# T5 attention with a squared-ReLU feed-forward on one core: x of pairs 4 and 5 through the DMA transpose, x of four later pairs in one transfer, and a new table of due times

## The chip, the core and the metric

The kernel runs on one core of one Trainium2 chip. The metric is the device time of one execution in microseconds. The version before takes 360.38 us, the median of three runs (360.12 to 360.55). One profiled execution stands beside them. The kernel was scheduled by hand to within a few microseconds of its matmul work, so changes of a fraction of a per cent are what is discussed here.

## What is computed

```
scores = q @ k.T / 8                       # 8 batches, 8 heads, 576 positions, head size 64
scores = scores + bias_table[bucket(|i - j|)]
attn   = softmax(scores)                   # over the keys
x      = (attn @ v), heads put side by side  -> 4608 x 512
out    = relu(x @ w_in) ** 2 @ w_out       # w_in 512 x 2048, w_out 2048 x 512, out float32
```

Inputs and output are float32 in DRAM; inside, the kernel works in fp16 with float32 accumulation.

## The kernel before

**Attention** goes by pairs of heads. There are 32 pairs; pair p belongs to batch p // 4, so pairs 4 to 7 are batch 1, and pairs 16, 20, 24 and 28 are the first pairs of batches 4 to 7. A pair loads q and k (POOL issues those DMAs, L368), turns them so that the head size lies on partitions, and multiplies them (`scores_of`, L815 and L822; the last 64 keys in L1012). ACT takes the exponential (L997, L831, L1022), and DVE multiplies by a table of exponentiated bias (L728). `values` (L741) then multiplies by v on TensorE (L754, L761), takes a reciprocal of the row sums (L775) and writes the normalized x on DVE (L780). It does so in two parts: part 0 has three tiles of 128 positions, part 1 two (the last one half full). In batch 0 alone the parts have two and three tiles.

**x has to be turned once more**, because the feed-forward multiplies with the 512 features on partitions. There are two ways in the kernel:

- For batches 0 and 1 `x_turn` (L1068) does it on TensorE. It has five operations, one for each tile of 128 positions. Each makes four transposes (L1078), one for each pair of the batch, into one PSUM bank, and a copy on ACT (L714) or DVE (L716) brings the bank into `xt_sb`. Such an operation needs the x of all four pairs.
- From batch 2 on (`DT_X = 2`) `values` itself issues a DMA transpose from SP's queue behind each of its two parts (L793 to L799). It writes straight into `xt_sb`. There are 48 of these, two for each of 24 pairs.

**The feed-forward** goes by nine groups of 512 rows (`GT`), in `layers`. A group's first layer reads `xt_sb` (L1501, in some groups partly by seven products instead of eight, L1378; group 0 by halves, L1451). ACT and DVE apply the squared ReLU (L1530, L1540). The second layer (L1204) does with seven products of half size what would be eight. A batch has 576 rows, so group 1 (rows 512 to 1023) needs the last 64 rows of batch 0 and the first 448 rows of batch 1. Its first layer may start only when all pieces of x named in `xt_ready[1]` have landed.

**The order of the work** is set by a planner inside the kernel (`Plan.schedule`, L191). Every operation has a number, in the order in which it is made, a list of what it depends on, buffers, a price in ns and a due time. The planner walks through a modelled execution; on each engine it picks the operation that can start first, and of several that can start at once the one with the smallest due time. The instructions are then issued to each engine in that fixed order. The string `DUES` (L67 to L120) overrides the due times of about 500 operations by number (L1573 to L1575). TensorE, ACT, DVE, POOL and the queue of SP each run their list strictly in order.

Of the kernel before, what the change touches and what calls it, by code (L numbers as in the profile page):

```python
# [11 lines left out]
FP16 = mybir.dt.float16  # L12
# [21 lines left out]
DT_X = 2  # L34
RELU_DVE = 0
# [32 lines left out]
0:1620 2:1057 4:1180 10:1374 14:10158 16:8662 20:10687 22:11516 35:2669 52:4535 56:9455 58:7112 60:7916 68:10815  # L68
74:10190 76:8720 78:12175 80:15005 82:13645 84:11550 86:23580 88:22110 92:24205 94:15740 96:16365 98:5160
100:26470 102:20015 104:19280 106:20750 108:14380 110:12910 112:21375 116:24830 118:22845 120:25735 122:32560  # L70
124:28912 126:37814 128:33913 130:40556 132:37611 138:53077 140:59257 142:35621 144:56022 146:62717 148:55174
150:59442 152:57545 154:56196 156:78298 158:57307 160:47495 164:49300 166:57988 168:69667 170:53855 172:74624
174:52573 193:116470 196:82589 198:68922 200:82230 202:292670 204:92367 210:87027 214:113261 242:100900
274:107211 276:119523 282:111649 290:106325 430:180789 436:197382 438:250584 444:209080 447:199176 470:192471
496:220887 498:225440 500:217803 527:29842 528:27168 534:53417 535:54369 538:56772 539:54354 540:60089 541:57850
542:7652 548:11111 550:8057 553:10032 568:12045 573:14473 575:15118 578:13413 585:16397 598:18178 614:21930
615:22689 616:22710 619:25948 625:25934 626:29177 634:23911 635:22035 636:22362 641:27192 649:28075 653:35265
656:34983 659:28843 664:42977 671:36147 678:37745 680:37557 682:43619 692:26764 696:49415 697:77051 699:42404
702:50396 705:51612 720:49430 721:146141 729:49109 730:59630 737:58473 739:111790 740:23251 741:24529 742:22846
744:25455 746:43041 747:124773 752:20617 755:43976 760:57060 761:54459 763:47620 771:47854 772:51849 773:129366  # L80
775:48374 777:46047 779:42740 786:66406 790:62872 792:31486 798:74992 801:49147 803:61538 804:55525 805:65305
806:194213 811:64571 812:62370 829:55606 830:74008 852:80804 854:85724 858:82674 863:81398 867:83698 874:72663
878:82910 883:85677 887:68893 888:207137 892:91006 896:88734 901:75364 903:73448 907:85605 911:73890 914:95939
917:76004 918:96413 925:94537 928:89870 945:67990 946:80414 948:75587 950:67245 952:88819 981:78127 982:78920
989:89488 994:92890 1005:93482 1011:89302 1013:90614 1019:95353 1024:114015 1035:101128 1038:99231 1067:119398
1069:117655 1074:124317 1076:120546 1079:118292 1080:136781 1082:115304 1085:100217 1093:126164 1095:128386
1096:97962 1097:128084 1100:102019 1102:129303 1106:127303 1111:130634 1115:118676 1117:129752 1122:120899
1126:119722 1129:110655 1133:124513 1137:123585 1144:114735 1147:117401 1150:142607 1157:209061 1164:124814
1165:253316 1169:130366 1171:133696 1172:149728 1176:135925 1183:146398 1194:116773 1197:107201 1199:106444
1208:140568 1213:119988 1224:117192 1225:240653 1227:122452 1229:112062 1231:277079 1238:133898 1243:133447  # L90
1254:138298 1268:150015 1273:137361 1285:154673 1286:123911 1288:156589 1293:149183 1295:161760 1296:165255
1298:142184 1301:173103 1312:157945 1316:169960 1321:175132 1325:162782 1330:167105 1334:162397 1341:151871
1344:137808 1345:138678 1348:147955 1352:157383 1356:151613 1359:151655 1360:174070 1363:153941 1366:162394
1370:184432 1372:192411 1374:187205 1376:185782 1386:146887 1397:164889 1402:166927 1413:155368 1418:169097
1422:177129 1426:136922 1427:173973 1432:178937 1443:158230 1444:228059 1446:153250 1454:349338 1457:167384
1462:177010 1473:176589 1476:172655 1478:176540 1479:185500 1501:179718 1503:182250 1508:190343 1510:203005
1516:199512 1523:171343 1527:190195 1531:205450 1534:183047 1536:208496 1540:207327 1545:200160 1549:203926
1556:207389 1560:184812 1567:203181 1571:198563 1576:198936 1578:201689 1581:208725 1588:225038 1591:244956
1603:175092 1612:196147 1617:183544 1628:195491 1631:212780 1633:224396 1635:217128 1639:225517 1658:189178
1663:191367 1672:210715 1677:211394 1678:227828 1687:192179 1688:203407 1693:209674 1707:227130 1716:219200  # L100
1718:226066 1720:214927 1723:238316 1725:237862 1728:238618 1729:194614 1734:211389 1739:224576 1742:244441
1745:212768 1746:235036 1749:211379 1751:243380 1755:236163 1760:242402 1764:254767 1771:248608 1775:252775
1782:239688 1786:236303 1789:231239 1793:249320 1796:251032 1802:260804 1805:258837 1807:172350 1813:226190
1814:235218 1816:224638 1818:216417 1827:236087 1846:221877 1848:237634 1849:253782 1850:245738 1851:256163
1857:244985 1864:350531 1873:233367 1879:227859 1880:228340 1887:245518 1892:255737 1894:258771 1906:230982
1908:244937 1909:248019 1910:253722 1918:154960 1922:256387 1935:266967 1937:267963 1942:269901 1944:270198
1945:286508 1947:271205 1950:269272 1952:274893 1953:233383 1954:247394 1961:255388 1965:270026 1968:262833
1970:276519 1971:279751 1973:284808 1974:278869 1977:272671 1979:274936 1982:284959 1983:151931 1986:262274
1990:265311 1994:275938 1995:280226 1998:288907 2001:273934 2005:256374 2012:286562 2015:251154 2021:296191
2023:289373 2032:263421 2035:260356 2037:274391 2038:264239 2039:282682 2040:278169 2046:280738 2051:286535  # L110
2062:261514 2068:261952 2069:255665 2076:272292 2092:273655 2095:275739 2099:272928 2122:278929 2125:285022
2126:284839 2127:277523 2128:283181 2129:280296 2141:295193 2150:297975 2152:299266 2157:306028 2159:311561
2165:290995 2172:302812 2174:303364 2179:301973 2181:308356 2184:293569 2187:309532 2190:275380 2194:309550
2195:309256 2196:313265 2198:307321 2201:313552 2203:313106 2209:317667 2212:290350 2213:188745 2224:72572
2226:310220 2227:311767 2231:283869 2236:304785 2240:302563 2247:295321 2250:302190 2255:330506 2265:310664
2267:319453 2269:317532 2272:318235 2274:329364 2275:326890 2277:115300 2280:314656 2283:317429 2285:321158
2290:321339 2292:326200 2298:327300 2299:329122 2301:330181 2303:327337 2308:319851 2310:335293 2316:334886
2319:48914 2320:295724 2323:330893 2325:333730 2330:336969 2332:335768 2335:331254 2338:89017 2341:324215
2342:327990 2345:329056 2349:323549 2350:329628 2352:330954 2367:348049
# [146 lines left out]
def mm(n):  # L266
    return n / 2.4 + 2.5
# [11 lines left out]
def kernel(  # L279
# [425 lines left out]
    xt_ready, x_last, xt_half, every_slot = {}, {}, {}, []  # L705
# [35 lines left out]
    def values(p, part, qt0, nq, pb, deps, T, after):  # L741
# [48 lines left out]
        if b >= DT_X:  # L790
            c = (b % XB) * S + 128 * qt0
            t = P.add(
                {"SP": 1320.0},  # L793
                lambda: io(
                    nc.sync.dma_start_transpose(
                        out=xt_sb[:, hp, c : c + 128 * nq].rearrange("p (t d) -> p t d", d=128), in_=xs[xb.slot][:, qt0 : qt0 + nq, :].rearrange("p t d -> p (t d)")
                    )
                ),
                [o, x_last.get((hp, 1 - part))] + xt_free(b * S + 128 * (qt0 + nq)), [xb], T - 2000,  # L799
            )  # L800
            t = x_last[hp, part] = P.land((128 * nq, 25.0), [t], [xb], SPARE[1])
            end = b * S + min(128 * (qt0 + nq), S) - 1
            for g_ in range((b * S + 128 * qt0) // GT, end // GT + 1):
                xt_ready.setdefault(g_, []).append(t)
# [114 lines left out]
    def pair(p):  # L919
# [116 lines left out]
        else:  # L1036
# [28 lines left out]
            values(p, part, qt0, nq, pb, bands + list(exps.values()), T, after) for part, qt0, nq in ((0, 0, 3), (1, 3, 2))  # L1065
        ]

    def x_turn(b, norms):  # L1068
        xb = [x_bufs[4 * b + hp] for hp in range(4)]
        T = nominal(4 * b + 3)  # L1070
        for qt in range(5):
            n = 128 if qt < 4 else 64
            bank = Buf(r_g)

            def tr(qt=qt, bank=bank):
                ps = g_ps[bank.slot].bitcast(FP16)
                for kk in range(4):
# [531 lines left out]
```

## Time and profile before

| | before |
|---|---|
| median of three runs | 360.38 us (360.12 to 360.55) |
| the profiled execution: its time | 360.5 us |
| its span, first to last instruction | 358.7 us |
| TensorE busy (PE) | 346.4 us, 97% of the span |
| VectorE (DVE), ScalarE (ACT), GpSimd (POOL) | 297.5, 272.6, 170.6 us |
| granted TensorE clock | 1.0 throughout |
| x transposes on TensorE (L1078) | 40 |
| x transposes by DMA (L795) | 48 |

The profiled execution's time is 1.8 us more than its span; that rest lies outside of the first and the last instruction. "PE" is the matmul pipeline, "PEld" the load of weights into it, "SPq" the queue of SyncE. A line number is a line of the kernel before. Ends of matmuls are modelled, so the distance between the starts of neighbours tells more of a matmul's price than its own duration.

### The profile page before, as it was taken

The page shows a single profiled execution, that of the slowest core. Times are in us where ns is not written, and L with a number is a line of the kernel's source. Part 1 is how long each engine was busy: PE and PEld are TensorE (multiplying, and loading weights), DVE is VectorE, ACT ScalarE, POOL GpSimd, SP SyncE. Part 2 cuts the span into 40 slices and gives each one's busy share as a digit, 9 for nine tenths or more (in the row PEclk, how much of TensorE's full clock was granted, in tenths as well). Part 3 has the DMA queues.
Part 4 walks back from the last instruction along what each step waited for, and adds up shares of the span by engine and source line. Part 5 has one row for each costly group of instructions (what it writes and reads, how often), then busy time and mean ns, then how long its engine had stood idle before and what let it go on. Part 6 is the DMA issues. An engine that isn't in the chain of part 4 may idle for free.

```text
span 358.7 us, 10742 instructions
## 1 busy us (share of the span) xinstructions
PE 346.4 (97%) x4290; PEld 262.0 (73%) x4290; DVE 297.5 (83%) x673; ACT 272.6 (76%) x435; POOL 170.6 (48%) x289
## 2 busy tenths in 40 slices
PE   3988999999999999999999999999999999999996
PEld 3666788775587558877788568755867887888885
DVE  4888999666996799768896899798988798899993
ACT  4898997589966988678976887689889833899830
POOL 8886679698995896158478456221000000000000
PEclk9999999999999999999999999999999999999999
DMA  9999999999999999799999999863410032010023
GB/s 172 151 147 198 193 150 154 190 156 192 175 130 165 223 158 112 119 163 198 84 134 164 186 126 133 150 121 72 61 44 15 18 97 68 27 63 33 23 66 117
DMA packets 162210, 44.37 MB, mean 124 GB/s; under 512 B 145520, under 2 KB 162160, under 8 KB 162160
## 3 DMA queue, kind: packets, MB, share of 16 engines
q0 software_dynamic: 74208, 14.53, 54.6%
q1 hardware_dynamic: 87696, 28.86, 44.3%
q8 instruction: 33, 0.54, 0.6%
q10 hardware_dynamic: 256, 0.30, 0.3%
q14 instruction: 17, 0.14, 0.1%
HBM read 36.94 MB, written 9.44 MB: 129 GB/s over the span
## 4 chain that ended last, share of the span: by engine, by line
PE 88%; DMA 7%; POOL 2%; ACT 1%; issue 1%; DVE 0%; POOLq 0%
PE f L1204 31%; PE f L1501 20%; PE f L761 10%; PE st L815 8%; PE f L1378 7%; DMA w_in_sb<-in_moe_w_in_dram 5%; PE f L1451 3%; PE st L1378 3%; PE f L754 3%; PE st L1012 2%; DMA ks<-in_k_dram 2%; POOL va L368 2%; PE f L822 1%; PE f L1078 1%; POOL ks L368 0%
## 5 line engine op out<-in xcount | busy, mean ns | idle before, releaser
L997 ACT ACTIVATE pt<-st 128x1024 f16<-128x1024 f32 x112 | 111.1, 1031 | 23.0 <-PE st L815 22.8
L1501 PE MATMUL f<-xt,w_in_sb 128*128 128x512 f16 (+4 forms) x416 | 77.2, 330 | 0.0
L728 DVE TENSOR_TENSOR pt<-pt,tb_sb 128x512 f16<-128x512 f16 (+3 forms) x108 | 61.9, 581 | 12.6 <-ACT pt L997 9.3
L368 POOL DMA_DIRECT2D ks<-in_k_dram x79 | 55.9, 719 | 15.1 <-DMA kt<-ks 10.4
L1204 PEld LDWEIGHTS <-g 128*128 128x128 f16 x576 | 55.1, 98 | 7.6 <-issue 0.8
L368 POOL DMA_DIRECT2D qs<-in_q_dram x79 | 55.5, 712 | 8.1 <-DMA qt<-qs 6.2
L1530 ACT ACTIVATE rt<-f 128x512 f16<-128x512 f32 x80 | 47.3, 608 | 14.1 <-PE f L1501 12.7
L1501 PEld LDWEIGHTS <-w_in_sb 128*128 128x128 f16 x416 | 37.1, 98 | 26.7 <-issue 2.5
L761 PE MATMUL f<-va,pt 128*128 128x65 f16 x1280 | 53.2, 193 | 0.3 <-DMA va<-in_v_dram 0.3
L761 PEld LDWEIGHTS <-pt 128*128 128x128 f16 x1280 | 49.8, 97 | 1.3 <-issue 0.5
L1204 PEld LDWEIGHTS <-s 128*128 128x128 f16 x432 | 41.1, 98 | 5.8 <-issue 0.8
L1232 DVE SCALAR_TENSOR_TENSOR y<-f,y 128x512 f32<-128x512 f32 (+1 forms) x48 | 31.8, 665 | 12.5 <-PE f L1204 11.7
L815 PE MATMUL st<-qt,kt 64*128 64x512 f16 (+1 forms) x288 | 40.4, 361 | 1.0 <-DVE qt L716 0.6
L1540 DVE TENSOR_TENSOR g<-rt 128x512 f16<-128x512 f16 x80 | 34.3, 433 | 6.2 <-ACT rt L1530 5.3
L1204 PE MATMUL f<-wt,g 128*128 128x256 f16 x288 | 35.6, 273 | 0.0
L754 PE MATMUL f<-vm,pm 128*128 128x130 f16 x160 | 35.5, 222 | 0.0
L1204 PE MATMUL f<-w_out_sb,s 128*128 128x256 f16 x288 | 35.3, 273 | 0.0
L1204 PE MATMUL f<-w_out_sb,g 128*128 128x256 f16 x288 | 34.7, 273 | 0.1
L780 DVE TENSOR_TENSOR x<-f,r 128x384 f16<-128x384 f32 (+1 forms) x64 | 30.9, 485 | 0.9
L645 POOL CAST va<-f 128x512 f16<-128x512 f32 x24 | 16.7, 702 | 30.8 <-DMA f<-in_v_dram 17.5
L974 POOL COPY kz<-kt 64x64 f16<-64x64 f16 x55 | 19.4, 354 | 20.2 <-DMA kt<-ks 17.1
L831 ACT ACTIVATE pt<-f 128x256 f16<-128x256 f32 x64 | 22.9, 404 | 5.9 <-PE f L822 4.5
(112 smaller groups left out, 532.4 us busy)
## 6 DMA issues: line engine op xcount, KB each, us to landing
out_dram<-y SPq DMA_DIRECT2D x34, 256.0 KB, 2.8
f<-in_v_dram SPq DMA_DIRECT2D x24, 256.0 KB, 4.9
ks<-in_k_dram POOLq DMA_DIRECT2D x48, 64.0 KB, 5.2
qs<-in_q_dram POOLq DMA_DIRECT2D x48, 64.0 KB, 4.4
w_in_sb<-in_moe_w_in_dram POOLq DMA_DIRECT2D x4, 512.0 KB, 10.7
w_out_sb<-in_moe_w_out_dram POOLq DMA_DIRECT2D x4, 512.0 KB, 8.9
ks<-in_k_dram POOLq DMA_DIRECT2D x7, 144.0 KB, 5.6
qs<-in_q_dram POOLq DMA_DIRECT2D x7, 144.0 KB, 5.5
```

What stands on the lines that cost most here:

```text
L368: lambda: io(eng.dma_start(out=out_(), in_=in_())),
L728: io(nc.vector.tensor_tensor(out=a, in0=a, in1=t, op=MULT))
L754: nc.tensor.matmul(ps[:, i, :, :], pm[:, c : c + 128], vm[:, hp, :, 0:65], start=True, stop=False)
L761: nc.tensor.matmul(ps[:, i, e, :], pt[:, (2 * jt + e) * S + c : (2 * jt + e) * S + c + 128], va[:, jt, 2 * hp + e, 0:65], start=False, sto ...
L815: nc.tensor.matmul(banks[i][:, e, :], kt[rw[e], ts(jt, 128)], qt[rw[e], ds(q0, n)], start=True, stop=True)
L997: nc.scalar.activation(out=p5(pts[pb.slot])[:, jt, :, 0:512], in_=sets_ps[st.slot], func=EXPF, scale=SCALE)
L1204: nc.tensor.matmul(home[bf.slot][:, ts(s_, HALF)], left(c, s_), right(c), start=(c == 0 and (s_ == 0 or apart) and (own or i not in before ...
L1232: nc.vector.scalar_tensor_tensor(out=dst, in0=ps, scalar=OSC, in1=ys[y[plus].slot][:, cs], op0=MULT, op1=mybir.AluOpType.add,)
L1378: nc.tensor.matmul(ps()[:, ds(HALF * f + a, z - a)], left()[:, kk, ts(f, 128)], right(a, z)[:, kk, :], start=(first_ and f == 0 and a == 0 ...
L1501: nc.tensor.matmul(g_ps[bank.slot][:, a:z], w_in_sb[:, kk, ts(nt, 128)], xt_sb[:, kk, c : c + z - a], start=(kk == 0), stop=(kk == 3),)
L1530: io(nc.scalar.activation(out=rts[rb.slot], in_=g_ps[bank.slot], func=RELUF))
L1540: nc.vector.tensor_tensor(out=gs[gb1.slot][:, nt, :], in0=rts[rb.slot], in1=rts[rb.slot], op=MULT)
```

## The change

It has three parts.

1. Two sets of pair numbers are new: `X_DMA = (4, 5)` and `X_ONCE = (16, 20, 24, 28)`.
2. Pairs 4 and 5, the first two pairs of batch 1, send x through the DMA transpose as batches 2 to 7 do. `x_turn` turns the pairs that are left. In batch 1 these are two, and as an operation still fills a bank of four transposes, it takes two tiles at a time: three operations of 4, 4 and 2 transposes take the place of five of 4. In batch 0 nothing is different.
3. Pairs 16, 20, 24 and 28 issue one DMA transpose of all five tiles behind the part that comes second, instead of one of three tiles and one of two.

All due times that `DUES` overrides are new: 467 entries stand where 502 stood. As the change makes and removes operations, their numbers shift: by 2 to 8 within batch 1, by 4 behind it, and from pair 16 on step by step back to minus 4. Up to number 762 they are the same.

```diff
+X_DMA = (4, 5)
+X_ONCE = (16, 20, 24, 28)
...
         o = P.add({"DVE": dve(nq * 128)}, norm, [o], [bank, rb, xb], T - 2000)
-        if b >= DT_X:
-            c = (b % XB) * S + 128 * qt0
+        if p in X_ONCE:
+            if not part:
+                x_first[p] = o
+                return o
+        a_, n_ = (0, 5) if p in X_ONCE else (qt0, nq)
+        if b >= DT_X or p in X_DMA:
+            c = (b % XB) * S + 128 * a_
             t = P.add(
                 {"SP": 1320.0},
                 lambda: io(
                     nc.sync.dma_start_transpose(
-                        out=xt_sb[:, hp, c : c + 128 * nq]..., in_=xs[xb.slot][:, qt0 : qt0 + nq, :]...
+                        out=xt_sb[:, hp, c : c + 128 * n_]..., in_=xs[xb.slot][:, a_ : a_ + n_, :]...
                     )
                 ),
-                [o, x_last.get((hp, 1 - part))] + xt_free(b * S + 128 * (qt0 + nq)), [xb], T - 2000,
+                [o, x_first.get(p), x_last.get((hp, 1 if p in X_ONCE else 1 - part))] + xt_free(b * S + 128 * (a_ + n_)),
+                [xb], T - 2000,
             )
...
     def x_turn(b, norms):
-        xb = [x_bufs[4 * b + hp] for hp in range(4)]
+        turn = [hp for hp in range(4) if 4 * b + hp not in X_DMA]
+        xb = [x_bufs[4 * b + hp] for hp in turn]
+        k0, nk = turn[0], len(turn)
+        wide = 4 // nk
         T = nominal(4 * b + 3)
-        for qt in range(5):
-            n = 128 if qt < 4 else 64
+        for qt in range(0, 5, wide):
+            qts_ = range(qt, min(qt + wide, 5))
+            n = min(128 * wide, S - 128 * qt)
...
-                for kk in range(4):
-                    io(nc.tensor.transpose(ps[:, ts(kk, 128)], xs[xb[kk].slot][:, qt, :], id_sb))
+                for i in range(nk):
+                    for j, t_ in enumerate(qts_):
+                        io(nc.tensor.transpose(ps[:, i, ts(j, 128)], xs[xb[i].slot][:, t_, :], id_sb))
...
-            deps = [n_[0 if qt < (2 if b < HALVES else 3) else 1] for n_ in norms]
+            early = 2 if b < HALVES else 3
+            deps = [norms[hp][w] for hp in turn for w in range(2) if (qts_[0] < early if w == 0 else qts_[-1] >= early)]
```

A few of the due times that matter for what follows, by the operation's number (which is the same before and after for these): 590 and 594, the two sets of score products of part 0 of pair 2, 5300 before, 14785 and 15933 after; 760, the product with v of part 0 of pair 4, 57060 before, 70746 after; 763, that of part 1, 47620 before, 51633 after.

## The prediction

> **What bounds the kernel now.** I read the page's busy times first, then the busy times cut into three stretches, then the waits of TensorE, then the chain of work that ended last around the transposes that go, and at last the rows of the DMA transposes. The page:
>
> ```profile
> PE 346.4 (97%) x4290; PEld 262.0 (73%) x4290; DVE 297.5 (83%) x673; ACT 272.6 (76%) x435; POOL 170.6 (48%) x289
> ```
>
> TensorE is busy in nearly all of the span, and no other engine comes near. Three stretches (PE, weight load, DVE, ACT and POOL busy, granted clock, DMA):
>
> ```profile
> 0.00:34.33 34.33, 25.24 (x511) 19.02 (x511) 25.17 (x78) 27.93 (x46) 27.54 (x53) 1.00 1.32 166
> 34.33:355.49 321.16, 321.06 (x3780) 243.02 (x3780) 271.86 (x595) 244.69 (x390) 143.04 (x236) 1.00 0.97 119
> 355.49:358.70 3.21, 0.06 (x1) 0.00 (x0) 0.42 (x1) 0.00 (x0) 0.00 (x0) 0.98 0.48 161
> ```
>
> From 34.33 us to 355.49 us PE rests for 0.10 us of 321.16. That stretch is a list of matmuls one behind the other, at full clock; it becomes shorter only by instructions that go. Ahead of it PE rests for 9.1 us, behind it lie 3.2 us of reading, storing and landing. The waits of PE (total, times, longest):
>
> ```profile
> PE f L419 <- DMA id_sb<-c_id: 4.4, 1, 4.4
> PE f L1451 <- DMA w_in_sb<-in_moe_w_in_dram: 1.3, 1, 1.3
> PE f L947 <- ACT ex_sb L424: 1.3, 1, 1.3
> PE st L815 <- DVE qt L716: 0.6, 1, 0.6
> PE f L947 <- DVE qt L716: 0.4, 1, 0.4
> PE f L761 <- DMA va<-in_v_dram: 0.3, 1, 0.3
> PE st L815 <- ACT pt L864: 0.3, 1, 0.3
> ...
> ```
>
> All of them lie in the first 34 us. Behind the first there are 4.2 us that another order could at best win back.
>
> **Part by part: the transposes of batch 1.** The chain of work that ended last runs through all 20 of them (start, length, what); these are the pieces:
>
> ```profile
> 74.10 0.22 PE f L1078 x4
> ...
> 75.19 0.67 PE f L1078 x12
> ...
> 80.09 0.22 PE f L1078 x4
> ```
>
> 20 transposes cost 0.22 + 0.67 + 0.22 = 1.11 us, 0.056 us each. The change makes 4 + 4 + 2 = 10 instead of 20, in one stretch without any cover, so **-0.56 us** on the path.
>
> A rule speaks against this part: in the Trainium skill, "VectorE: DVE Perf Modes", section "Rules for kernel authors", a 128x128 transpose belongs on TensorE where PSUM may take the result, and its section on the three paths gives 390 ns there against 1309 ns for the DMA. By these figures ten would be 3.9 us of TensorE, seven times what the chain shows; the rule compares one transpose alone with another, and here TensorE is what is full. It is right on latency, which the second rival takes up.
>
> **The copies.** Five copies out of PSUM become three. In the stretch from 75 to 80 us DVE is busy for 2.52 us of 5 and ACT for 4.26; one of 512 columns takes 0.42 us on DVE or 0.59 us on ACT. Two less give about 1 us to engines that don't set the end: nothing. Were ACT the bound, it would be worth up to 1.2 us.
>
> **Four more DMA transposes** for pairs 4 and 5 go into SP's queue among the q and k transposes of batch 2. The rows of the existing ones:
>
> ```profile
> L795 SPq DMA_TRANSPOSE xt<-x x48: 1168/1206/2377, 89.7 to 298.6; - x48
> DMA to landing us min/median/max: 2.3/4.1/6.9
> ```
>
> Each holds SP for 1.2 us and waits there for its norm on DVE; the q and k transposes and stores behind it wait too. Between 55.35 + 1.34 = 56.7 us and 62.2 us SP's queue issues nothing, so the room is there. Who waits for those q and k transposes are scores of batch 2, and PE has other work meanwhile. I take nothing; without that cover it would be 4 x 1.2 = 4.8 us of delay at the worst.
>
> **One transfer instead of two** for pairs 16, 20, 24 and 28 takes four issues of 1.2 us off SP, which isn't a bound, and holds the x of part 0 back until part 1 is ready. What covers this are the other three pairs of the same batch, which the feed-forward needs as well: batch 4's first x transposes are issued at 169.8 us, the layer that reads them starts at 196.7 us. Nothing; without the cover one landing, 4.1 us (up to 6.9).
>
> **The due times** reorder each queue, and the trace of before can't show the new order. Above: a better order can win at most the 4.2 us of waits in the head. Below: it can lose a landing of 6.9 us of DMA if some matmul is put ahead of its data. Inside the full stretch it can also bring score products together. Four of these, two side by side on half the rows, take 0.54 us in the chain (70.91 us), where two plain matmuls of 512 columns take 2 x 0.225 = 0.45 (twelve in 2.70 us), so a set put right behind another saves about 0.09 us. The early numbers in the table hardly change (590 and 594 get new values; the loads of w_in keep theirs), so I leave the 1.3 us for w_in where it is. I take **-0.3 us**: a third of the 0.9 us of PE's two waits ahead of score products (0.6 and 0.3 us), the rows nearest to what is re-dued there, or three sets of scores brought together. In the Trainium skill, "TensorEngine Tiling (Array Packing)", under "Key Properties", a change of the tiling mode drains TensorE. That agrees with the 0.09 us above in kind and gives no figure.
>
> **The sum**: 360.5 - 0.56 - 0.3 = 359.64 us by the profiled execution's own time. This lies 0.12 us above the median of the runs shown, so the forecast for a median is **359.5 us**, 0.25% below 360.38. About 0.2%, 0.72 us, is what a measurement of this kernel can tell from no change.
>
> **Rivals.** *First: only the transposes go.* The due times win nothing, and the freed slots are all there is: 360.38 - 0.56 = 359.8 us, within 0.2%. It may also lose 0.5 us in small waits and end at 360.3. For it speaks that PE has no waits left after 34 us that an order could remove; against it that the whole table was laid anew.
>
> *Second, slower: x of pair 4 lands after the feed-forward's group 1 wants it.* In before the norms of pairs 4 and 5 are done by 62.6 us, and the first matmul on that group starts at 77.3 us, behind transposes and copies that take about 3.2 us from 74.1 us on. After, the product of pair 4's part 0 has the due time 70746 instead of 57060, 13.7 us more. I read this as a bound on how far it may move, if PE always has something more urgent. In the trace its norm ends at 58.0 us, so it would end at the latest near 58.0 + 13.7 = 71.7 us; with 1.2 us on SP behind at most one other transpose (1.2) and a landing of 4.1 to 6.9 us from the issue on, x is there between 75.8 and 79.8 us. The point from which it decides is 77.3 us: up to there PE's list is what it was; beyond, PE stands still, or does batch 2 early and has it missing later. The price is at most 79.8 - 77.3 = 2.5 us; I take 2.0 in its case, so 360.38 - 0.56 + 2.0 = 361.8 us. For it speaks that TensorE and a copy need about 0.9 us from x to `xt_sb` (75.03 to 75.9 us for a bank) where the DMA needs 4.1. Against it speaks that the g=0 second layer and batch 2's scores can be put in between.
>
> *The change does what it says* on the counts: 30 transposes on TensorE and 48 DMA transposes must appear. I see no way for it not to.
>
> **How the numbers follow.** Forecast 0.52 (358.3 to 359.66 us), first rival 0.20 (359.66 to 361.1), second 0.28 (above 361.1). So faster 0.52, same 0.20, slower 0.28. The predicted time is the likeliest case's, 359.5 us. For the range: the low end takes 1.5 us of the 4.2 us in the head, 360.38 - 0.56 - 1.5 = 358.3. The high end is the second rival at its bound without the transposes' gain landing elsewhere: 360.38 - 0.56 + 2.5 = 362.3; I take 362.2. That leaves a tenth out at each side.
>
> **What the changed profile would show.** Right: L1078's successor with 30 matmuls and 0.056 us each in the chain, PE without waits behind 34 us, the full stretch shorter by 0.6 to 0.9 us, the rest before and behind it alike. First rival: the stretch shorter by 0.5 and no less waiting ahead of it. Second rival: a wait of PE, or of its weight load, on a DMA into xt near 77 us, and the first matmul on group 1 later than 77.3 us. Wrong altogether would be a stretch that has the same instructions less ten and is longer by more than 1 us with no wait named, or a head that differs by more than 1.5 us.

## The result

The changed kernel takes **361.9 us**, the median of 21 runs (359.58 to 363.51), against 360.38 us for the kernel before in 21 runs beside them. The ratio is 1.0038 with a 95% interval of 1.002 to 1.0055: slower, by 0.4%. The forecast was 359.5 us, so the forecast change has the wrong sign. That the time lies inside the range of 358.3 to 362.2 is luck, as the second rival shows below.

The profiled execution of the changed kernel happens to be among its shortest: 360.38 us with a span of 358.6 us, as long as that of the kernel before (358.7). The loss can't be read from these two traces alone. I therefore take four more traces of the changed kernel and compare what all five have in common. In some executions of either kernel the granted clock falls for a few microseconds, which costs 1.7 us (last section). Where I pool runs, I therefore use those at full clock (a mean of 0.998 or more) and give means with 95% intervals.

### The profile page after: what moved, and what is told of

Same layout as the page of the kernel before. It is cut to its first block, busy times and chain, and to the rows that moved or that the text cites. A ratio compares the mean times of both kernels' runs of the same rounds, so it can differ in the third digit from the quotient of the medians.

```text
span 358.6 us, 10748 instructions
## 1 busy us (share of the span) xinstructions
PE 346.1 (97%) x4280; PEld 260.3 (73%) x4280; DVE 299.6 (84%) x676; ACT 271.0 (76%) x430; POOL 171.2 (48%) x287
## 4 chain that ended last, share of the span: by engine, by line
PE 77%; DMA 10%; POOL 6%; ACT 4%; issue 1%; SPq 1%; DVE 0%; POOLq 0%
PE f L1216 28%; PE f L1513 16%; PE f L759 9%; PE st L821 7%; PE f L1390 6%; DMA w_in_sb<-in_moe_w_in_dram 5%; PE f L1463 4%; PE st L1390 3%; PE f L752 3%; DMA kt<-ks 2%; POOL va L366 2%; DMA f<-in_v_dram 2%; PE st L1018 2%; POOL ks L366 1%; ACT g L1436 1%
## 5 line engine op out<-in xcount | busy, mean ns | idle before, releaser
L1513 PE MATMUL f<-xt,w_in_sb 128*128 128x512 f16 (+4 forms) x416 | 76.4, 330 | 0.0
L1513 PEld LDWEIGHTS <-w_in_sb 128*128 128x128 f16 x416 | 37.4, 98 | 27.0 <-issue 1.7
L1552 DVE TENSOR_TENSOR g<-rt 128x512 f16<-128x512 f16 x80 | 35.4, 453 | 8.7 <-ACT rt L1542 7.5
L752 PE MATMUL f<-vm,pm 128*128 128x130 f16 x160 | 35.5, 222 | 0.0
L980 POOL COPY kz<-kt 64x64 f16<-64x64 f16 x54 | 22.2, 413 | 21.4 <-DMA kt<-ks 18.6
L643 POOL CAST va<-f 128x512 f16<-128x512 f32 x24 | 15.7, 666 | 23.3 <-DMA f<-in_v_dram 11.4
L1171 DVE TENSOR_TENSOR s<-g,s 128x1024 f16<-128x1024 f16 x36 | 24.6, 695 | 0.0
```

Source lines behind the costliest of these rows:

```text
L752: nc.tensor.matmul(ps[:, i, :, :], pm[:, c : c + 128], vm[:, hp, :, 0:65], start=True, stop=False)
L1513: nc.tensor.matmul(g_ps[bank.slot][:, a:z], w_in_sb[:, kk, ts(nt, 128)], xt_sb[:, kk, c : c + z - a], start=(kk == 0), stop=(kk == 3),)
L1552: nc.vector.tensor_tensor(out=gs[gb1.slot][:, nt, :], in0=rts[rb.slot], in1=rts[rb.slot], op=MULT)
```

## The profile after

The busy times of the page, and the three stretches (PE, weight load, DVE, ACT, POOL, granted clock, DMA):

```profile
PE 346.1 (97%) x4280; PEld 260.3 (73%) x4280; DVE 299.6 (84%) x676; ACT 271.0 (76%) x430; POOL 171.2 (48%) x287
```

```profile
0.00:34.33 34.33, 25.65 (x515) 19.32 (x516) 25.64 (x82) 28.21 (x46) 27.35 (x52) 1.00 1.30 164
34.33:355.49 321.16, 320.43 (x3768) 240.95 (x3765) 273.52 (x595) 242.77 (x385) 143.86 (x236) 1.00 0.91 120
355.49:358.60 3.11, 0.00 (x0) 0.00 (x0) 0.42 (x1) 0.00 (x0) 0.00 (x0) 0.95 0.47 157
```

There are ten matmuls less, as the change says. But in the middle stretch, where PE rested for 0.10 us before, it rests for 0.73 us. The waits of PE (total, times, longest) name one that lies behind 34 us, where there was none before; it is the last one shown:

```profile
PE f L417 <- DMA id_sb<-c_id: 4.4, 1, 4.4
PE f L953 <- ACT ex_sb L422: 1.3, 1, 1.3
PE f L1463 <- DMA w_in_sb<-in_moe_w_in_dram: 0.9, 1, 0.9
PE f L885 <- DVE qt L714: 0.7, 1, 0.7
PE f L759 <- DMA va<-in_v_dram: 0.6, 1, 0.6
PE st L1018 <- POOL kz L980: 0.5, 1, 0.5
...
```

L1018 is the product with the last 64 keys (L1012 before), `kz` a copy that POOL makes from the turned k. The transposes on TensorE and by DMA, counted, and the landing of the latter:

```profile
L1089 PE MATMUL f<-id_sb,x x30: 219/219/230, 23.7 to 74.7; 128*128 128x128 f16 x30
```

```profile
L798 SPq DMA_TRANSPOSE xt<-x x48: 1174/1210/2283, 56.4 to 298.3; - x48
...
DMA to landing us min/median/max: 2.3/3.6/7.0
```

Now the chain that ended last, in order of time. In the kernel before it is made of matmuls alone from 34 to 174 us. In the changed kernel it leaves TensorE at 71.8 us and comes back at 103.8 us:

```profile
72.04 0.21 SPq L798
72.41 1.20 SPq L936
...
76.47 6.07 DMA f<-in_v_dram
82.60 0.26 POOL vm L643
...
86.45 3.56 DMA qs<-in_q_dram
90.01 8.59 DMA kt<-ks
...
102.71 1.04 POOL kz L980
103.80 0.42 PE st L1018 x2
```

Read it downwards: SP issues an x transpose of the new kind (L798), then a transpose of k (L936) and further loads; a load of v's tail (`f`, the last 64 positions) lands late; POOL casts it (`vm`) late; that makes POOL's next loads of q and k late, then the transposed k, then `kz`; and TensorE stands still. The wait is 0.48 us in this execution. The question for the experiments is whether this is the loss, and which of the three parts of the change brings it.

## Experiments

All the edited kernels here issue their instructions from a written-out list (operation number and engine) in place of the planner's choice, so that an order and a way of x can be combined freely. Their line numbers are some 97 higher than those of the changed kernel: L849 is its L752, L1115 its L1018, L1610 its L1513. The list replaces the planner:

```diff
-    for op in P.schedule():
+    for op in P.replay():
```

"Old order" is the list of the kernel before, "new order" that of the changed one. An instruction that one list lacks stands where its norms end. Letters in the expectations: Q the load on SP's queue, O the new order itself, T the late single transfer, C the clock, H the first 34 us, M the stretch from 80 to 120 us.

### One part alone, and one taken back

Four kernels ran on one chip, beside the kernel before: 360.31 us in 35 runs. Each ratio below is to the kernel before on the same chip, with its 95% interval.

**The changed kernel again.** Unchanged.

> The changed kernel once more, for its spread and for a second trace. Its profiled execution was as short as that of before (span 358.6 against 358.7 us), while its median is 1.5 us longer. Theory Q (SP's queue: the four new x transposes push q and k transposes of batch 2 back, and how long PE then stands still depends on when DMAs land in that run): median near 361.9 us, and a longer execution shows a wait of PE on kz or on qt and kt between 70 and 110 us. Theory O (the new order of everything else has no slack in other places): the wait of a longer execution lies elsewhere. Theory C (clock): no wait, but a granted clock below 1.0 in the longer execution.

361.38 us, ratio 1.0021 [0.9999, 1.0042]. The trace has other waits than the first one:

```profile
86.44 0.22 PE L752 MATMUL f<-vm,pm 128*128 128x130 f16 x1 [0.75 <-POOL vm L643]
118.10 2.10 PE L1513 MATMUL f<-xt,w_in_sb 128*128 128x512 f16 x9 [0.17 <-DMA xt<-x]
```

So it is not one late transfer, but several that end close to the time at which TensorE needs them. I call that TensorE's edge. The clock is 0.999 in this execution, so theory C doesn't explain it.

**Old order, only the single transfers (X_ONCE).**

```diff
-X_DMA = (4, 5)
+X_DMA = ()
```

> Every instruction in the order of before, only the x of pairs 16, 20, 24 and 28 in one transfer. Theories Q and O both: 360.4 us, no difference above 0.2%. Against both (theory T: the late single transfer is what costs): 361.4 to 361.9 us.

360.65 us, 1.001 [0.9984, 1.0036], and 359.8 us as the median of its 6 runs at full clock, as the kernel before. No wait of PE between 34 and 345 us. T's 361.4 us lies just inside the interval, but nothing in the trace speaks for it: holding back part 0 of four pairs leaves no wait.

**Old order, only pairs 4 and 5 by DMA.**

```diff
-X_ONCE = (16, 20, 24, 28)
+X_ONCE = ()
```

> Every instruction in the order of before, only pairs 4 and 5 send x by DMA, each transpose put into SP's queue where its norm ends, and batch 1's transposes on TensorE are three operations. Theory Q: slower than before by 1 to 2 us, with a wait of PE on kz, kt or qt near 75 to 100 us. Theory O: 359.8 us, ten transposes less and nothing else.

360.28 us, 1.0007 [0.9982, 1.0032]. Q's loss of 1 to 2 us is not there. Whether the ten transposes bring their 0.56 us can't be told: a ratio of 0.9984 lies inside the interval. There is one new wait, of the kind of my second rival, but for batch 2 and 42 us later:

```profile
119.08 1.24 PE L1610 MATMUL f<-xt,w_in_sb 128*128 128x512 f16 x5 [0.68 <-DMA xt<-x]
```

**New order, pairs 4 and 5 on TensorE as before.** The same edit as for the second kernel, with the new list.

> Every instruction in the order of the changed kernel, but pairs 4 and 5 turned on TensorE again by five operations, so that SP's queue has four entries less between 56 and 73 us. Theory Q: back to 360.4 us plus the 0.56 us of the ten transposes, 360.5 to 361.0. Theory O: 361.9 plus 0.56, so 362.4 us.

361.47 us, 1.0028 [1.0008, 1.0049]. This is about the time of the changed kernel, without its DMA transposes of pairs 4 and 5, and lies between Q's 361.0 and O's 362.4. So the order, with the single transfers, is enough for the loss; Q is at most a part. The trace has no wait for `vm` or `kz`, but one of 0.82 us for x of batch 2 at 118.56 us: here too another chain is last.

### Where in the order

Four kernels on a second chip; before: 359.95 us in 23 runs. Both ways of x are on. The list of one kernel holds up to 34 us, that of the other afterwards:

```diff
-SEQ = new
+SEQ = old up to 34 us + what is left, as in new
```

> Both x paths of the change are on. Up to 34 us every engine goes in the order of before, from there on in the order of the changed kernel. Theory H (the new order's first 34 us is what costs, by waits for v, q and w_in in the head): 359.8 to 360.3 us, as before. Theory M (the new order's stretch from 80 to 120 us is what costs: DMA chains that end right at PE's edge there): 361.3 us, as the changed kernel, with 0.5 to 1.0 us of waits of PE between 80 and 120 us.

362.16 us, 1.0047 [1.0022, 1.0072]. Two waits in the middle:

```profile
53.01 1.91 PE L1560 MATMUL f<-xt,w_in_sb 128*128 128x256 f16 x16 [1.05 <-DVE x L875]
...
88.16 0.22 PE L849 MATMUL f<-vm,pm 128*128 128x130 f16 x1 [1.07 <-POOL vm L740]
```

The first one, at 53 us, stands in no other trace.

```diff
-SEQ = new
+SEQ = new up to 34 us + what is left, as in old
```

> Both x paths of the change are on. Up to 34 us the order of the changed kernel, from there on the order of before. Theory H: 361.3 us. Theory M: about 360.2 us, as the order of before with pairs 4 and 5 on DMA had (360.28), with one wait near 119 us at the most.

360.94 us, 1.0015 [0.9989, 1.0042]. The kernel with the old head has the whole loss, where H asked for none. So H falls as the cause: the new order of what is behind 34 us is enough. The other kernel is not decided; its interval holds both no loss and the whole of it, and its trace has a wait of 0.95 us for `vm`. On the same chip the two kernels of the comparison were profiled once more each:

> The kernel before once more, for a second trace. Theory M: no wait of PE between 34 and 345 us, as in the first trace. Theory H says nothing of that stretch, but expects less rest of PE in the first 34 us than in the changed kernel's traces (8.7 and 9.2 us up to 40 us).

360.59 us; PE busy for 40.00 of the 40 us from 80 to 120.

> The changed kernel once more, for a third trace. Theory M: waits of PE of 0.5 to 1.0 us in all between 80 and 120 us, of some DMA or of POOL. Theory H: more rest of PE in the first 40 us than before.

361.75 us; waits of 0.46 us for `vm` at 87.25 us and of 0.44 us for `kz` at 105.18 us. In the first 34.33 us PE rests for 9.1 and 8.2 us in the two traces of the kernel before, for 8.7 to 9.7 us in the five of the changed one.

### Taking a late transfer forward, and back

Four kernels on the first chip again; before: 359.97 us in 35 runs.

**The load of v's tail earlier.** In SP's part of the list of the changed kernel (190 and 193 are the two loads of v's tail, 244 that of v's next pair, 975 and 1005 transposes of k, 798 an x transpose):

```diff
-798S 975S 193S 1005S 244S 190S 905S
+798S 190S 975S 193S 1005S 244S 905S
```

> The changed kernel in its own order, one instruction moved: SyncE issues the load of the second part of v's tail (the one that goes out at 75.9 us in the changed kernel) four places earlier in its queue, directly behind the x transposes and ahead of two q/k transposes and two other loads. That load then goes out near 72.5 us, the other one near 74.3, and the last of the two lands 1.6 us earlier. Theory M (chains of transfers that end just at TensorE's edge between 80 and 120 us, pushed back by SyncE's queue): TensorE's wait for the cast of v's tail at 86 to 88 us (0.5 to 0.75 us in two traces of the changed kernel) and the one for the last keys near 104 us (0.44 to 0.48) go, at most the one for x of batch 2 at 118 us is left; 360.6 to 361.0 us, 0.4 to 0.8 below the changed kernel in this call. Theory O (the new order costs as such, everywhere): no difference from the changed kernel, 361.3 to 361.6.

361.23 us, 1.0034 [1.0008, 1.006], no less than the changed kernel beside it (360.93). The wait for `vm` shrank from 0.83 to 0.47 us, but did not go. The trace offers a reason: POOL waits 1.65 us for the transposed k at a `kz` copy ahead of the casts, and that transpose of k goes out later by the one place that the load has taken. M's 360.6 to 361.0 us did not come. That the next link took over is argued from this one trace.

**The tail's second load later, in the kernel before** (999 is a transpose of q, 923 a store):

```diff
-193S 999S 923S 1158S
+999S 923S 193S 1158S
```

> The reverse: the kernel before with its own order and its own way of x, one instruction moved: SyncE issues the second load of v's tail behind a q/k transpose and a store that stood after it, so near 75.9 us in place of 73.3, where the changed kernel has it. Theory M: a wait of 0.3 to 1.0 us of TensorE for the cast of v's tail at 86 to 88 us, which the kernel before does not have; 360.3 to 360.9 us, 0.3 to 0.9 above it. Theory O: as the kernel before, 360.0 to 360.3.

360.76 us, 1.0011 [0.9986, 1.0035]: not decided. I had misread which load is which. In the kernel before the load at 73.27 us is that of v's next pair, and the tail's second one goes out at 76.84 us; the edit moved it to 79.34 us. The cast was then done at 84.38 us, and TensorE's first product on it starts at 85.60 us, so 1.2 us were left and no wait appears.

**Both ways of x in the old order**, the change without its due times, with the list of the kernel before:

> The change without its due times: both new ways of x (pairs 4 and 5 through the DMA transpose with three operations on TensorE for the other two, four later pairs in one transfer), and every other instruction in the order of the kernel before. All theories that lay the loss on the new order: as the two ways measured alone, 360.0 to 360.6 us, within 0.1% of the kernel before. If the two ways cost only together: 361 us or more.

360.21 us, 1.0017 [0.9986, 1.0048], as expected if the loss lies in the order. The trace has one wait, of 0.75 us for `vm` at 86.03 us.

**The changed kernel** as the measure:

> The changed kernel as it is, on the same chip, as the measure for the first of these runs: 361.3 to 361.8 us.

360.93 us, 1.002 [0.9995, 1.0044], less than the 361.3 expected; waits of 0.83 us for `vm` and 0.28 us for x of batch 2.

### The last link of the chain

Four series on a third chip; before: 360.42 us in 35 runs. First, on POOL, the second cast of v's tail (195) moves ahead of the first (192):

```diff
-192G 242G 246G 232G 195G
+195G 192G 242G 246G 232G
```

> The changed kernel in its own order, one GpSimd instruction moved: the second of the two casts of v's tail (at 84.9 to 87.0 us in the traces of the changed kernel, behind the first cast, which waits 0.9 to 1.6 us for its load, and behind three other instructions of GpSimd) now stands ahead of the first, in the time in which GpSimd waits for that load anyway. TensorE's value products need both casts, so they are ready some 2 us sooner: near 83.0 to 85.0 us, against 86.3 us, when TensorE comes to them. Theory M: TensorE's wait for that cast at 86 to 88 us (0.5, 0.75 and 0.8 us in three traces) is gone; what is left between 80 and 120 us is 0.1 to 0.5 us for the last keys and x of batch 2; 360.4 to 360.8 us, 0.4 to 0.8 below the changed kernel. If a later edge takes over, the waits for the last keys near 104 us and for x near 118 us grow by as much and the time stays at 361.1 to 361.5.

> The same kernel a second time, since the spread of one series (1.5 us) is as large as the difference looked for: 360.4 to 360.8 us by theory M, 361.1 to 361.5 us if a later edge takes over.

360.73 us, 1.0022 [1.0002, 1.0043], and 360.78 us, 1.0018 [0.9991, 1.0045]. The wait for `vm` is gone in both traces. What is left, in the first one (the second has 0.45 us for `kz` at 104.40 us):

```profile
105.88 0.42 PE L1115 MATMUL st<-qt,kz 128*128 128x288 f16 x2 [0.44 <-POOL kz L1077]
120.47 2.10 PE L1610 MATMUL f<-xt,w_in_sb 128*128 128x512 f16 x9 [0.64 <-DMA xt<-x]
```

At full clock the two series together take 360.81 +/- 0.37 us (21 runs), all series of the changed kernel 361.19 +/- 0.26 (47 runs). The difference of 0.4 us goes the way M said, at the lower end of its 0.4 to 0.8, but its interval reaches zero, and beside the changed kernel on this chip (361.05) it is 0.2.

> The change without its due times a second time: both new ways of x, everything else in the order of the kernel before. 360.0 to 360.5 us if the loss is in the new order; its trace showed the same wait for the cast of v's tail (0.75 us), paid for by a sum of TensorE that is 1.4 us smaller, so by theory M it varies between 359.3 and 360.5 with that wait.

360.12 us, 0.9994 [0.9969, 1.0018]: no loss in the series. Its profiled execution is one of the long ones, 362.13 us, with a wait of 1.98 us, the longest of all between 34 and 90 us:

```profile
84.69 0.42 PE L1115 MATMUL st<-qt,kz 128*128 128x288 f16 x2 [1.98 <-POOL kz L1077]
```

> The changed kernel as it is, on the same chip, as the measure of the first two: 361.0 to 361.5 us, with waits between 80 and 120 us of 0.5 to 1.1 us in all.

360.94 us, 1.0032 [1.0006, 1.0058]. The waits between 80 and 120 us come to 1.65 us, above the 0.5 to 1.1 expected, with the longest one for `vm` of all:

```profile
88.38 0.22 PE L752 MATMUL f<-vm,pm 128*128 128x130 f16 x1 [1.62 <-POOL vm L643]
```

### An attempt at a better kernel

Both ways of x, old order, and the links that were late in its two traces put first, on a fourth chip; before: 359.91 us in 23 runs.

```diff
-190S 975S 916S 244S 1033S 1035S 193S 1003S
+190S 975S 916S 193S 1033S 1035S 244S 1003S
...
-192G 220G 222G 224G 226G 246G 228G 977G 978G 230G 232G
+192G 220G 222G 224G 977G 978G 226G 195G 246G 228G 230G 232G
```

> Both new ways of x, the order of the kernel before, and the links that ended last in its two traces (a wait of 0.75 us for the cast of v's tail at 86 us in one, of 1.98 us for the last keys at 84.7 us in the other) moved forward: SyncE issues the second load of v's tail before the load of v's next pair, which takes its old place; GpSimd casts it before the cast of that next pair, and makes the two last-key copies ahead of six other instructions. Theory M (the x transposes push SyncE's queue back, TensorE waits where the chains through it end): no wait of over 0.4 us between 80 and 90 us, TensorE's busy sum stays at 345.0 to 345.7 us, 359.2 to 359.8 us, 0.3 to 0.9 below the kernel with both ways and below the kernel before. If a later edge takes over: a wait of as much at 95 or 116 us (the next last keys, x of batch 2) and 360.0 to 360.4 us.

> The same kernel a second time, for the spread of one series: 359.2 to 359.8 us by theory M, 360.0 to 360.4 us if a later edge takes over.

361.59 us, 1.0035 [1.0007, 1.0062], and 361.03 us, 1.0026 [0.9998, 1.0055]. The waits at 84 and 86 us are gone, but the next last keys wait, 0.29 us in the first trace and in the second:

```profile
98.06 0.66 PE L1115 MATMUL st<-qt,kz 128*128 128x288 f16 x2 [2.25 <-POOL kz L1077]
```

"A later edge takes over" was right in kind, but the times are above its 360.0 to 360.4 us. A part of that is the clock: it fell in 11 of the 24 runs, and the 13 at full clock have a mean of 360.5 us. None of the kernels beats the one before by more than the measurement can tell.

## Why the prediction was wrong

**What the runs add up to.** At full clock: the kernel before 359.88 +/- 0.13 us (108 runs); the kernels with one or both ways of x whose order behind 34 us is the old one, 360.29 +/- 0.32 (44 runs); those with the new order there, 361.22 +/- 0.21 (64 runs, the changed kernel among them; the kernels with single instructions moved are left out). Chip by chip it is the same picture: 0.15 to 0.7 us above the kernel before with the old order, 0.8 to 1.5 with the new one. So the new ways of x brought nothing or cost up to 0.8 us, and the new due times cost 0.9 us, give or take 0.4. I had -0.56 and -0.3 us.

**The step that failed** is the pair of assumptions by which TensorE stays full behind 34 us: "Who waits for those q and k transposes are scores of batch 2, and PE has other work meanwhile. I take nothing", and for the due times "a third of the 0.9 us of PE's two waits". I looked for what a new order could win in the head (4.4 us with a row of 0.2 that I left out, not 4.2) and priced the loss only as a bound (6.9 us for a landing). What I did not do is measure, for each transfer, how long before its reader it lands. A reading went wrong with it: I found room in SP's queue up to 62.2 us, but only the first of the four new transposes is issued in it (56.43 us in the first trace). The second goes out at 62.90 us, and the last two keep the queue until 72.2 us, ahead of a transpose of k and the loads of v's tail:

```profile
69.35 2.89 SPq L798 DMA_TRANSPOSE xt<-x  x2
```

The trace of before would have shown the margins. POOL before, from 80 us on (start, length, what, idle before):

```profile
80.29 0.77 POOL L974 COPY kz<-kt 64x64 f16<-64x64 f16 x2
81.01 0.60 POOL L368 DMA_DIRECT2D ks<-in_k_dram  x1
81.61 0.77 POOL L368 DMA_DIRECT2D qs<-in_q_dram  x1
83.09 0.40 POOL L645 CAST vm<-f 64x256 f16<-64x256 f32 x1 [0.72 <-DMA f<-in_v_dram]
```

```profile
86.10 0.23 PE L754 MATMUL f<-vm,pm 128*128 128x130 f16 x1
```

The second cast of v's tail is done at 83.49 us (the first was done at 75.7), and TensorE reads it at 86.10 us: a margin of 2.6 us. POOL in the fifth trace of the changed kernel:

```profile
82.96 0.23 POOL L980 COPY kz<-kt 64x64 f16<-64x64 f16 x1 [2.98 <-DMA kt<-ks]
83.45 0.59 POOL L366 DMA_DIRECT2D qs<-in_q_dram  x1 [0.25 <-issue]
85.27 0.50 POOL L643 CAST vm<-f 64x256 f16<-64x256 f32 x1 [1.23 <-DMA f<-in_v_dram]
85.72 0.59 POOL L366 DMA_DIRECT2D ks<-in_k_dram  x1
86.31 0.85 POOL L643 CAST va<-f 128x512 f16<-128x512 f32 x1
87.12 0.77 POOL L366 DMA_DIRECT2D qs<-in_q_dram  x1
87.93 0.40 POOL L643 CAST vm<-f 64x256 f16<-64x256 f32 x1
```

In the new order POOL waits for k's transpose, then for the first part of the tail, and the second part's cast stands behind three other instructions. It is done at 88.33 us; TensorE was there at 86.76. In the first trace the same cast is done at 85.54 us and read at 85.82: the margin is 0.3 us, so a landing that takes a little longer is enough for a wait. From 80 to 120 us, PE busy in the two:

```profile
80.00:120.00 40.00, 40.00 (x449) 26.41 (x448) 31.43 (x74) 33.08 (x54) 33.65 (x54) 1.00 1.87 173
```

```profile
80.00:120.00 40.00, 38.35 (x438) 25.43 (x438) 30.06 (x69) 32.46 (x52) 32.51 (x55) 1.00 1.63 169
```

Over the five traces of the changed kernel this stretch loses 0.48, 0.98, 0.91, 1.13 and 1.65 us, 1.03 on average; in the two of the kernel before nothing is lost.

**Ten transposes less, -0.56 us: the price of one is right, the gain isn't seen.** In the first trace of the changed kernel the ten start at 74.22 us and the next product at 74.78 us, so they take the 0.056 us each that I had:

```profile
74.22 0.72 PE L1089 MATMUL f<-id_sb,x 128*128 128x128 f16 x10
74.78 1.04 PE L1216 MATMUL f<-wt,g 128*128 128x256 f16 x8
```

PE's busy sum falls from 346.36 us in the first trace of the kernel before to 345.86 us on average of the four traces of the changed kernel at full clock, by 0.50. That looks like the ten transposes, but such sums can't be compared so closely. Early in the head the same instructions are slower, although the clock column reads 1.00 there. Where this ends differs between executions. Twelve 96x96 transposes of q or k in the kernel before:

```profile
12.74 0.69 PE L947 MATMUL f<-id_sb,qs 96*64 96x96 f16 x12
14.70 0.45 PE L947 MATMUL f<-id_sb,qs 96*64 96x96 f16 x12
```

In the second trace of the changed kernel:

```profile
7.83 0.69 PE L953 MATMUL f<-id_sb,qs 96*64 96x96 f16 x12
10.93 0.45 PE L953 MATMUL f<-id_sb,qs 96*64 96x96 f16 x12
```

The trace with the largest sum of all (348.93 us, the first with the cast moved) still takes 0.69 us for twelve at 17.18 us; the one with the smallest (344.97 us, the first with both ways in the old order) takes 0.45 us from 11.04 us on. So a part of the 0.50 us may be the head of that one execution; how much isn't shown.

In the same four traces PE rests longer by 0.88 us from 80 to 120 us (the fifth left out here), by 0.18 from 34 to 80, 0.18 before and 0.11 behind. With the -0.50 the sum is +0.85 us, and the mean span is 359.57 against 358.72. So in these traces the waits more than use up the gain. By the runs at full clock the loss is larger, 361.19 against 359.88, 1.3 us: the first profiled execution of the kernel before took 360.5 us, 0.6 more than the mean of its runs. In the old order PE's sum was even 345.4 us on average (three traces with both ways of x at full clock), 0.5 less than in the new one; I have not found out by what.

**Four more DMA transposes: "nothing" was wrong, "4.8 us at the worst" held.** The second load of v's tail is issued at 76.84 us without them, in the kernel before:

```profile
76.84 0.63 SPq L368 DMA_DIRECT2D f<-in_v_dram  x1
```

With them, in the second trace of both ways in the old order, at 80.83 us, behind a transpose of k that waits for its load:

```profile
77.30 3.48 SPq L1033 DMA_TRANSPOSE kt<-ks  x1
80.83 0.63 SPq L463 DMA_DIRECT2D f<-in_v_dram  x1
```

In the first trace it was 78.26 us. Not all of this is the new transposes: without them the load goes out at 77.45 us in the second trace of the kernel before and at 78.51 with the single transfers alone. Measured back from the moment at which TensorE comes to the first product on it, the load is issued 9.3, 8.8 and 8.1 us ahead in these three traces, and 7.0, 6.7, 6.8 and 6.7 us ahead in the four with the new transposes and the old order behind 34 us; the second of these would be 4.7 without a wait of 1.98 us just before. So they use up 1.1 us of the margin at the least, and what the margin was differs too: 2.6, 3.1 and 1.4 us in the three traces without them. Of the two executions with both ways, the one with a wait of 0.75 us is as long as the first of the kernel before (span 358.6), the one with 1.98 us is longer by 1.7 us; the medians of their series show no loss.

**The second rival: right in sign, wrong in place.** That its 361.8 us is so near to the measured 361.9, and that the range holds it, is luck: x of pairs 4 and 5 was in time. The last of their transposes is issued by 72.2 us, and the first matmul on group 1 starts at 76.4 us, 0.9 us earlier than before. What came late were transfers of the next batch, out of the same queues.

**The single transfer, the counts**: as predicted, no wait, and 30 and 48 instructions. The copies were not measured by themselves. What the prediction named as a sign of being wrong altogether did not come; all the waits have names.

**What stays open.** Shown is that the new order behind 34 us brings the loss. That the waits from 80 to 120 us are the larger part of it is argued from the traces: the experiments that took one of them away won 0.4 us with an interval that reaches zero, or nothing, and in each another wait was left or came up. The waits behind 34 us are 1.2 us longer than before on average (0.88 + 0.18 + 0.11); less the 0.56 us of the transposes that leaves 0.6 us of the 1.3 that the runs show. Where the rest lies, in PE's sum, in the head or elsewhere, isn't settled: the four traces of the changed kernel at full clock differ by 0.4 us in the one and by 1.0 us in the other.

## What to carry to other kernels

Where one engine is full, a change that takes work off it is worth only what the margins of its feeders allow: list, for each chain of transfer, cast and copy, how long it ends before its reader, and compare the smallest margin (here 2.6 us in the first trace of the kernel before) with the delay that the change puts on the queue (here 1.1 us at the least and up to 4 us). A cast or a copy that stands in an in-order queue behind a wait is as late as that wait. Putting the cast that was ready first ahead took away the wait for it in both traces here, but then the next chain was last, so one link mended is not yet time won. When margins are near zero, one trace shows one sample: between 80 and 120 us the same kernel waited at three different places in five traces.

## What was unexpected in the hardware

In 8 of 20 traces the granted clock falls once before the last matmuls, soon after TensorE had stood still. The busy times and the clock (third column from the end) in stretches of 5 us, in the fifth trace of the changed kernel, after a wait of 1.79 us that ended at 22.80 us:

```profile
20.00:25.00 5.00, 3.14 (x52) 2.17 (x48) 2.79 (x12) 4.19 (x9) 3.02 (x4) 0.94 1.19 138
25.00:30.00 5.00, 5.00 (x71) 3.53 (x70) 4.37 (x11) 3.64 (x7) 4.96 (x9) 0.72 1.34 153
30.00:35.00 5.00, 4.77 (x112) 3.71 (x109) 4.74 (x17) 5.00 (x12) 2.54 (x13) 1.00 1.24 206
```

That is 5 x (0.06 + 0.28) = 1.7 us of full speed lost. In stretches of 1 us from 24 to 28 us the clock reads 0.68, 0.50, 0.50 and 0.61, which is half speed for 3.4 us. In the other traces it is 1.7 us too: 5 x 0.34 in one stretch at 0.66, or 5 x (0.22 + 0.12). The waits just before were of 1.17 to 2.25 us. But waits of 1.98 and 1.68 us in other traces, and the one of 1.62 us at 88.38 us in this one, had no such consequence, so length alone does not decide it, and no run here shows what does. It happens in both kernels (after 1.17 us in the kernel before), in 42 of 151 runs of the kernel before beside the experiments and in 11 of 58 of the changed one, so it does not explain their difference. If the wait is what sets it off, a wait of 1 to 2 us is now and then dearer than its own length. The Trainium skill, "TensorE: Matmul & The Clock Gate", section "Part 1: The HAM clock gate", has the clock at half rate for windows of about 3.4 us after an idle window of that length. Half of 3.4 is the 1.7 us seen here; the idle times here are shorter than the page's, and there the measurement decides.
